# Folding beta1 in as a row-sum multiple on VectorE, broadcasting three constant rows on GpSimd, and reordering a planned schedule

## The chip, the cores and the metric

The kernel runs on one core of a Trainium2 chip. The core has TensorE (PE in the profile), VectorE (DVE), ScalarE (ACT), GpSimd (POOL), and SyncE (SP), which here only issues transfers. The metric is the device time of one execution in microseconds, and the time of a kernel is the median of its runs.

## The reference

A windowed attention with a few always-visible "sink" keys feeds a token-mixing and channel-mixing MLP block. B is 4, H 8, S 768, D 64, so the model width is 512. The window is 128 keys, there are 4 sinks, and the MLP's hidden width is 2048.

```python
scores = scale * np.matmul(q, k.transpose(0, 1, 3, 2))
keep = is_sink | in_window
a = np.exp(...); a = a / (np.sum(a, axis=-1, keepdims=True) + 1e-09)
x = np.matmul(a, v)                      # -> (B, S, H * D)

a1 = alpha1 * x + beta1
tok = np.einsum('ts,bsd->btd', w_tok, a1)
u = x + lam * tok
a2 = alpha2 * u + beta2
ch = np.maximum(a2 @ w_ch1, 0.0) @ w_ch2
out = u + lam * ch
```

The change concerns `lam * tok`. Written out, lam times w_tok applied to (alpha1 x + beta1) is w_tok applied to (lam alpha1 x), plus the row sum of w_tok at row t times (lam beta1). `lam`, `alpha1` and `beta1` are vectors over the 512 channels, so on chip they are needed as a row repeated in all 128 partitions.

## The kernel before, in words

**Work.** The four batches run one after the other. Each batch has attention (transposed q and k, scores S, exponentials E, the product pv with v, normalised into x), token mixing (tok, giving u in place in x), an affine and a transpose (uT), a first MLP product with relu (h, hT), and a second one (ch), added into x and written out. Rows are tiled by 128 (six tiles r or ti); the 2048 hidden channels are tiled by 128 (16 tiles fi). While the MLP of batch b runs, the attention of batch b+1 runs between its matmuls. Only batch 0 has its attention alone, at the start; there it is also split in two halves of four heads (G = 0 and 1).

**Order.** Nothing is ordered by a scheduler on the chip. A `Plan` gathers tasks (`add`): each has a priority, the engines that may run it with a cost in ns, the tasks it comes after, and the buffers it uses. `emit` walks a model of the five engines and of the DMA rings, always takes the task that can start first (ties by priority), gives it an engine and a buffer, and writes its instructions. So each engine gets a fixed sequence, and an instruction that has to wait holds up all that follow it on its engine. A task with `port=True` is kept from overlapping with GpSimd work when it runs on VectorE. Where the model sees TensorE idle before 36 us, it fills the gap with idle matmuls (`idle`, line 308). `since` is an earliest time in the model; `ROWS` is 7500 ns.

**Constants.** `lam`, `alpha1` and `beta1` are loaded as one row each (lines 329 to 331). `spread_rows` (line 937) multiplies alpha1 and beta1 by lam on GpSimd within one partition (lines 938 and 940), and `spread` (line 756) repeats each of the three rows over 128 partitions by an fp32 matmul with a column of ones (line 759) and a copy out of PSUM. The results are `lam_b`, `la1_b` and `lb1_b`.

**Where beta1 enters.** For batch 0 GpSimd multiplies each half of x by `la1_b` (`half`, line 691), and tok adds one more matmul, the row sums of w_tok (`rsr`) against the row lam beta1 (`lb16`, line 790). The row sums come from ScalarE's cast of w_tok with an accumulator (line 737), are put in a column (line 741), turned by a matmul (line 744) and copied to `rsr` (line 753). For batches 1 to 3 GpSimd does two passes over each x tile: times `la1_b` (line 701), plus `lb1_b` (line 704); the result xh goes straight into tok.

**Lines to follow.** Casts and copies go through `copy` (lines 315 on ScalarE and 317 on the other two). `trans` (line 500) casts a q or k tile, transposes it on TensorE (line 521) and copies it out to qkT. `scores` gives S (line 612, a bias added by line 607), E (line 627) and on VectorE a mask (line 636). `pv` gives line 659 and the normalisation (lines 682 and 683). `tok` is line 786, its addition into x line 795, its cast to u16 the copy again. `cast_w2` multiplies the second MLP weight by `lam_b` (line 768), on VectorE or GpSimd. The first MLP weight is loaded from GpSimd's queue (line 480).

Of the kernel before, what the change touches and what calls it, by code (L numbers as in the profile page):

```python
# [13 lines left out]
P_ = 128  # L14
# [83 lines left out]
class Task:  # L98
    def __init__(self, prio, engs, fn, after, uses, mode, lands, port):
        self.prio, self.engs, self.fn, self.uses = prio, engs, fn, uses  # L100
        self.mode, self.lands, self.port = mode, lands, port
        self.needs = [a for a in after if a and a.seen is None]
        self.ready = max([0.0] + [a.seen for a in after if a and a.seen is not None])
        self.then = []
        self.seen = None


class Plan:


    def __init__(self, pools, homes, fill):
        self.tasks = []

        self.fill = fill
        self.pools = pools
        self.homes = {k: [0.0] * n for k, n in homes.items()}
        self.busy = {k: [False] * n for k, n in homes.items()}

    def add(self, prio, engs, fn, after=(), uses=(), mode=None, lands=None, port=False,
            since=0.0):  # L120


        t = Task(prio, engs, fn, after, uses, mode, lands, port)
        t.ready = max(t.ready, since)
        for b in uses:
            b.left += 1
        for a in t.needs:
            a.then.append(t)
        self.tasks.append(t)
        return t  # L130

    def emit(self):
        order = sorted(range(len(self.tasks)), key=lambda i: (self.tasks[i].prio, i))
        rank = {id(self.tasks[i]): r for r, i in enumerate(order)}
        waiting = {id(t): len(t.needs) for t in self.tasks}
        open_ = []
        free = {e: 0.0 for e in (PE, ACT, DVE, POOL, SP)}
        rings = Rings()

        def admit(t):  # L140
            bisect.insort(open_, (rank[id(t)], t), key=lambda x: x[0])

        def end(t, seen):
            t.seen = seen
            for b in t.uses:
                b.left -= 1
                b.freed = max(b.freed, seen)
                if b.left == 0:
                    self.busy[b.kind][b.home] = False
                    self.homes[b.kind][b.home] = b.freed  # L150
            for o in t.then:
                o.ready = max(o.ready, seen)
                waiting[id(o)] -= 1
                if not waiting[id(o)]:
                    admit(o)

        def pick():
            best = None
            for r, t in open_:
                at = t.ready  # L160
                for b in t.uses:
                    if b.t is None and b.home is None:
                        homes = [h for h, x in zip(self.homes[b.kind], self.busy[b.kind]) if not x]
                        n = sum(1 for o in t.uses if o.t is None and o.kind == b.kind)
                        if len(homes) < n:
                            at = None
                            break
                        at = max(at, sorted(homes)[n - 1])
                if at is None:
                    continue  # L170
                for e in t.engs:
# [3 lines left out]
                    key = (at_e, r, at_e + t.engs[e])  # L175
                    if best is None or key < best[0]:
                        best = (key, t, e)
            return best

        for t in self.tasks:  # L180
            if not waiting[id(t)]:
                admit(t)
# [3 lines left out]
        done = 0  # L186
        while done < len(self.tasks):
            best = pick()
            if best is None or landing <= best[0][0]:
# [5 lines left out]
            (start, r, _), t, e = best  # L195
            open_.remove((r, t))
            for b in t.uses:
                if b.t is None:
                    spare = [i for i, x in enumerate(self.busy[b.kind]) if not x]
                    b.home = min(spare, key=lambda i: self.homes[b.kind][i])  # L200
                    self.busy[b.kind][b.home] = True
                    pool, shape, dtype = self.pools[b.kind]
                    b.t = pool.tile(b.shape or shape, b.dtype or dtype,
                                    tag=f"{b.kind}_{b.home}", bufs=1, name=b.name)
            until, idle, took = self.fill
            n = int((start - max(free[PE], 900.0)) / (took if free[PE] > 4500.0 else 110.0))
            if e == PE and free[PE] < until and n > 0:
                free_d = [(h, i) for i, (h, x) in enumerate(zip(self.homes["d"], self.busy["d"])) if not x]
                if free_d and min(free_d)[0] <= free[PE]:
                    h = min(free_d)[1]  # L210
                    idle(self.pools["d"][0].tile(
                        [P_, 512], FP32, tag=f"d_{h}", bufs=1, name=f"idle{done}"), n)
                    self.homes["d"][h] = start
                    mode = None
            t.fn(e)
# [12 lines left out]
            t.at = (e, start, free[e])  # L228
            done += 1
# [6 lines left out]
        self.ends = free  # L236


@with_exitstack
def kernel(  # L240
# [85 lines left out]
    rsr = Buf("tmp", [P, NR, P], FP16, "rsr")  # L326
    lb16 = Buf("tmp", [P, DM], FP16, "lb16")
# [15 lines left out]
    ones_r = const.tile([1, P], FP32, name="ones_r")  # L343
    nc.vector.memset(ones_r, 1.0)

    rcol = const.tile([P, S // P, P], FP16, name="rcol")
    nc.vector.memset(rcol, 0.0)
# [62 lines left out]
    SPREAD = -790  # L410
# [12 lines left out]
    def load_qk(p, b, hp, t, wait=None):  # L423
        bf = nat[b, hp, t] = Buf("nat", None, None, f"nat{b}_{hp}_{t}")
        src = (q, k)[t][b, 2 * hp : 2 * hp + 2]
        if b < XB:
            src = src.rearrange("h (p r) d -> p h (r d)", p=P)
            done["nat", b, hp, t] = add(
                p, {SP: 480}, lambda e: nc.sync.dma_start(bf.t, src), [wait], [bf], lands=(16, 72))
# [214 lines left out]
    def pv(p, b, r, G):  # L644
# [52 lines left out]
        elif G == 1:  # L697
            tmp = Buf("tmp", None, None, f"tmp{b}_{r}")

            def m1(e):  # L700
                nc.gpsimd.tensor_mul(tmp.t, bx.t.rearrange("p h d -> p (h d)"), la1_b)  # L701

            def m2(e):
                nc.gpsimd.tensor_add(bh.t, tmp.t, lb1_b)  # L704

            a = add(p + 0.2, {POOL: 1270}, m1, [a, done["x", b, r, 0], done["la1"]], [bx, tmp])
            done["xh", b, r, 1] = add(p + 0.3, {POOL: 1305}, m2, [a, done["lb1b"]] + prior, [tmp, bh])
# [17 lines left out]
    def cast_wtok(p, ti):  # L725
# [3 lines left out]
        pr = Buf("d", [P, P], FP32, f"rs{ti}")  # L729
        col = Buf("rec", [P, 1], FP32, f"rc{ti}")  # L730
# [5 lines left out]
        def cast(e):  # L736
            nc.scalar.activation(
                w.t.rearrange("p r i -> p (r i)"), src.t[:, ti % 3, :], AF.Copy, accum_out=col.t)

        def mid(e):  # L740
            nc.vector.tensor_copy(rcol[:, ti, 0:1], col.t)

        def row(e):
            nc.tensor.matmul(pr.t, rcol[:, ti, :], iden, start=True, stop=True)

        c_ = add(p, {ACT: 850}, cast, [done["wtn", ti]], [src, w, col])
        a = add(p + 0.1, {PE: 330}, tr, [c_], [w, pt])
        a = done["wtokT", ti] = add(
            p + 0.2, {DVE: 560, ACT: 810}, lambda e: copy(e, wtokT[:, :, ti * P : (ti + 1) * P], pt.t),
            [a], [pt])  # L750
        a = add(p + 0.25, {DVE: 146}, mid, [c_], [col])
        a = add(p + 0.3, {PE: 60}, row, [a], [pr])
        done["rs", ti] = add(p + 0.4, {DVE: 200, ACT: 280},
                             lambda e: copy(e, rsr.t[:, ti, :], pr.t), [a], [pr, rsr])

    def spread(p, name, src, o):

        pt = Buf("d", None, None, f"b_{name}")
        a = add(p, {PE: 900}, lambda e: nc.tensor.matmul(pt.t, ones_r, src, start=True, stop=True),  # L759
                [done.get(name)], [pt], since=ROWS)  # L760
        done[name] = add(p + 0.1, {DVE: 600, ACT: 600}, lambda e: copy(e, o, pt.t), [a], [pt])
# [15 lines left out]
    def tok(p, b, ti):  # L777
# [5 lines left out]
        def mm(sis):  # L783
            def f(e):
                for si in sis:
                    nc.tensor.matmul(  # L786
                        pt.t, wtokT[:, si, ti * P : (ti + 1) * P], hs[si].t,
                        start=(si == 0), stop=(si == NR - 1 and b > 0))
                if b == 0 and sis[-1] == NR - 1:
                    nc.tensor.matmul(pt.t, rsr.t[:, ti, :], lb16.t, start=False, stop=True)  # L790
# [10 lines left out]
        for sis in ((0, 1, 2, 3), (4, 5)) if b == 0 and ti < 2 else (range(NR),):  # L801
            after = [done["wtokT", ti], a, b == 0 and done["rs", ti], b == 0 and done["lb1"]] + [
                done["xh", b, r, G] for r in sis for G in ((0, 1) if b == 0 else (1,))]
            a = add(p, {PE: 215 * (len(sis) + (b == 0 and sis[-1] == NR - 1))}, mm(sis), after, [pt] + [hs[si] for si in sis] + [rsr, lb16] * (b == 0 and sis[-1] == NR - 1))
        done["tok", b, ti] = a
        before = [done["xh", b, ti, G] for G in ((0, 1) if b == 0 else (1,))]
        a = done["u", b, ti] = add(p + 0.1, {DVE: 690}, ua, [a] + before, [pt, bx])
# [129 lines left out]
    def spread_rows():  # L937
        done["la1"] = add(-880, {POOL: 1270}, lambda e: nc.gpsimd.tensor_mul(rows[1], rows[1], rows[0]),
                          since=ROWS)
        a = done["lb1b"] = add(-878, {POOL: 1270}, lambda e: nc.gpsimd.tensor_mul(rows[2], rows[2], rows[0]),  # L940
                               since=ROWS)
        z = add(-990, {POOL: 400}, lambda e: nc.gpsimd.memset(lb16.t, 0.0), [], [lb16])
# [134 lines left out]
```

## Time and profile before

The median of 13 runs is 272.6 us (270.18 to 274.27). The profiled execution took 274.27 us, and its span from the first to the last instruction is 272.6 us, so 1.67 us lie around the span; that the span equals the median is chance.

| what | value |
|---|---|
| span, profiled execution | 272.6 us |
| time of that execution | 274.27 us |
| median of 13 runs | 272.6 us |
| TensorE busy | 262.2 us, 96% |
| VectorE busy | 144.2 us, 53% |
| ScalarE busy | 133.6 us, 49% |
| GpSimd busy | 109.3 us, 40% |
| granted TensorE clock, mean | 0.972 |
| first h matmul (end of batch 0's attention and token mixing) | 50.3 us |
| TensorE idle before 50 us / after | about 5.1 us / 1.1 us, and the end |

To read it: "busy" of an engine counts its own instructions; a busy TensorE includes the idle matmuls that the kernel itself puts there (72 of them, 6.8 us) and time at a lower clock, where the same matmul takes longer. A wait on an engine is told with what released it. The chain of waits goes back from the last instruction through whatever each step waited for.

### The profile page before, as it was taken

How to read it: one execution, taken by the hardware profiler on the slowest of the kernel's cores; microseconds unless marked ns; L12 is line 12 of the kernel's file. 1: busy time of each engine (PE TensorE's matmuls, PEld its weight loads, DVE VectorE, ACT ScalarE, POOL GpSimd, SP SyncE). 2: the span in 40 equal slices, each digit the busy share in tenths (PEclk: the TensorE clock that was granted, in tenths of full speed). 3: DMA queues.
4: the chain of work that ended last, by engine and by line, in shares of the span. 5: the costliest groups of instructions: out<-in, count | busy, mean ns of one | idle time of the engine just before them, and what ended most of it. 6: DMA issues, size and time to landing. Idle time of an engine off the chain costs nothing.

```text
span 272.6 us, 4880 instructions
## 1 busy us (share of the span) xinstructions
PE 262.2 (96%) x1904; PEld 141.3 (52%) x1904; DVE 144.2 (53%) x299; ACT 133.6 (49%) x222; POOL 109.3 (40%) x124
## 2 busy tenths in 40 slices
PE   7599999999999999899999999999999999999994
PEld 6235465665655554455655444555654445665441
DVE  4336666777888744448996144279853344000222
ACT  3266877578755222688960023787700135773000
POOL 5741893692684472025886602004846000000000
PEclk9856999999999999999999999999999999999998
DMA  6999999908972897789956999200011233000221
GB/s 208 328 203 379 381 287 256 165 2 223 317 155 46 169 261 163 138 192 242 185 76 142 253 166 216 76 2 0 2 38 42 96 89 84 2 0 0 81 77 77
DMA packets 85485, 39.65 MB, mean 145 GB/s; under 512 B 73419, under 2 KB 79571, under 8 KB 85462
## 3 DMA queue, kind: packets, MB, share of 16 engines
q1 hardware_dynamic: 83328, 37.24, 54.8%
q0 software_dynamic: 2112, 2.10, 4.5%
q8 instruction: 15, 0.25, 0.4%
q14 instruction: 8, 0.07, 0.1%
q10 hardware_dynamic: 22, 0.01, 0.0%
HBM read 29.63 MB, written 6.29 MB: 132 GB/s over the span
## 4 chain that ended last, share of the span: by engine, by line
PE 92%; DMA 3%; DVE 2%; issue 1%; SPq 0%; ACT 0%; DVEq 0%; ACTq 0%
PE ch L893 30%; PE h L869 30%; PE tok L786 11%; PE S L612 5%; PE pv L659 4%; DMA nat<-in_k_dram 3%; PE tp L521 2%; PE S L607 2%; PE pv L652 1%; DVE E L636 1%; PE b_lb1b L759 1%; PE b_la L759 1%; PE b_lam L759 1%; PE sk L560 1%; PE wT L734 1%
## 5 line engine op out<-in xcount | busy, mean ns | idle before, releaser
L869 PE MATMUL h<-uT,w1f 128*128 128x384 f16 x512 | 90.7, 326 | 1.1 <-ACT uT L813 0.9
L893 PE MATMUL ch<-w2f,hT 128*128 128x512 f16 x384 | 88.4, 379 | 0.0
L869 PEld LDWEIGHTS <-w1f 128*128 128x128 f16 x512 | 47.4, 98 | 33.6 <-issue 4.8
L893 PEld LDWEIGHTS <-hT 128*128 128x128 f16 x384 | 36.4, 98 | 41.0 <-issue 0.2
L875 ACT ACTIVATE hT<-h 128x384 f16<-128x384 f32 x93 | 45.7, 491 | 21.2 <-PE h L869 21.0
L627 ACT ACTIVATE E<-S 128x1024 f16<-128x1024 f32 (+1 forms) x42 | 40.6, 1003 | 10.2 <-PE S L612 5.8
L904 DVE TENSOR_TENSOR x<-x,ch 128x512 f32<-128x512 f32 x24 | 16.5, 687 | 50.4 <-PE ch L893 49.8
L701 POOL TENSOR_TENSOR tmp<-x,la_b 128x512 f32<-128x512 f32 x18 | 25.5, 1419 | 39.3 <-DVE x L683 37.1
L315 ACT CAST u<-x 128x512 f16<-128x512 f32 x18 | 11.1, 617 | 58.4 <-DVE x L795 58.4
L786 PE MATMUL tok<-xh,wtokT 128*128 128x512 f16 x144 | 34.7, 379 | 0.0
L795 DVE TENSOR_TENSOR x<-x,tok 128x512 f32<-128x512 f32 x24 | 16.5, 688 | 22.3 <-PE tok L786 19.0
L704 POOL TENSOR_TENSOR xh<-tmp,lb_b 128x512 f16<-128x512 f32 x18 | 25.5, 1414 | 1.3
L877 DVE TENSOR_SCALAR hT<-h 128x384 f16<-128x384 f32 x35 | 19.2, 554 | 11.7 <-PE h L869 11.4
L636 DVE TENSOR_TENSOR E<-E,maskn 128x1024 f16<-128x1024 f16 x25 | 23.8, 985 | 0.0
L317 POOL CAST vf<-vnat 128x512 f16<-128x512 f32 x18 | 12.2, 680 | 24.5 <-DMA vnat<-in_v_dram 22.7
L786 PEld LDWEIGHTS <-wtokT 128*128 128x128 f16 x144 | 13.8, 98 | 15.3
L683 DVE TENSOR_TENSOR x<-pv,rec 128x256 f32<-128x256 f32 x48 | 20.4, 424 | 1.7
L659 PEld LDWEIGHTS <-E 128*128 128x128 f16 x328 | 15.7, 98 | 6.3 <-issue 1.4
L659 PE MATMUL pv<-vf,E 128*128 128x65 f16 x328 | 18.7, 194 | 0.1
L317 POOL CAST n<-nat 128x768 f16<-128x768 f32 x17 | 14.0, 825 | 8.0 <-DMA nat<-in_q_dram 3.9
L317 POOL CAST u<-x 128x512 f16<-128x512 f32 x6 | 3.7, 622 | 27.1 <-DVE x L795 20.7
L612 PE MATMUL S<-qkT 64*128 64x256 f16 (+1 forms) x168 | 14.3, 283 | 0.0
(101 smaller groups left out, 215.7 us busy)
## 6 DMA issues: line engine op xcount, KB each, us to landing
nat<-in_q_dram SPq DMA_DIRECT2D x16, 384.0 KB, 6.5
nat<-in_k_dram SPq DMA_DIRECT2D x16, 384.0 KB, 3.8
out_dram<-x SPq DMA_DIRECT2D x24, 256.0 KB, 2.2
vnat<-in_v_dram SPq DMA_DIRECT2D x18, 256.0 KB, 3.4
wst_w<-in_moe_w_ch_dram SPq DMA_DIRECT2D x8, 512.0 KB, 9.1
wtn<-in_moe_w_tok_dram SPq DMA_DIRECT2D x6, 384.0 KB, 5.1
w1f<-in_moe_w_ch_dram POOLq DMA_DIRECT2D x4, 512.0 KB, 14.0
v<-in_v_dram SPq DMA_DIRECT2D x12, 128.0 KB, 5.5
```

The source lines that it names most:

```text
L317: engine[e].tensor_copy(o, i)
L612: nc.tensor.matmul(pv_[:, e_, i, :], o.t[rows, 2 * hp + 1, j * P : (j + 1) * P], o.t[rows, 2 * hp, j * P : j * P + w], start=not bias, sto ...
L627: nc.scalar.activation(eT.t, pS.t[:, :, 0 : n * w].rearrange("p e (i w) -> p e i w", i=n), AF.Exp, scale=scale)
L636: nc.vector.tensor_mul(ev, ev, m.to_broadcast(list(ev.shape)))
L659: nc.tensor.matmul(po.t[:, hl, :], eT.t[:, e_, off + i, c : c + P], vf[j][:, h, :], start=(r < 2 and n == 0), stop=(n == len(parts) - 1 an ...
L683: nc.vector.tensor_mul(bx.t[:, 4 * G : 4 * G + 4, :], po.t[:, :, 0:D], rec.t.to_broadcast([P, 4, D]))
L701: nc.gpsimd.tensor_mul(tmp.t, bx.t.rearrange("p h d -> p (h d)"), la1_b)
L704: nc.gpsimd.tensor_add(bh.t, tmp.t, lb1_b)
L786: nc.tensor.matmul(pt.t, wtokT[:, si, ti * P : (ti + 1) * P], hs[si].t, start=(si == 0), stop=(si == NR - 1 and b > 0))
L869: nc.tensor.matmul(ph.t, w1f[:, c, fi * P : (fi + 1) * P], bu.t[:, c, chk * NTOK : (chk + 1) * NTOK], start=(c == 0), stop=(c == NC - 1))
L875: nc.scalar.activation(bh.t[:, fi, :], ph.t, AF.Relu)
L893: nc.tensor.matmul(pc.t, bh.t[:, fi, nt * P : (nt + 1) * P], w2f[:, fi, :], start=(fi == 0), stop=(fi == NF - 1))
```

## The change

Seven things are changed at once.

1. The three rows are repeated over the partitions by GpSimd (`partition_broadcast`) in place of three matmuls and copies, and the products with `lam` are then taken on full tiles (128x512) by VectorE or GpSimd in place of single rows on GpSimd.
2. beta1 leaves the token product. The row-sum matmul and copies, `rsr`, `lb16` and the extra matmul of batch 0 go; for all batches a VectorE instruction per tile adds row sum times `lb1_b` to x in place (`beta`), after xh has been made from x. The addition of tok waits for it.
3. GpSimd's two passes per tile of batches 1 to 3 become one (`full`).
4. The cast of w_tok may run on VectorE too, with its accumulator; the row sums stay in fp32, one column per tile.
5. The q/k cast number 2 goes from GpSimd to VectorE; two of the first loads have longer transfer costs in the model (85 and 140 in place of 72); `LO`, from where the attention of batch 1 is spread over batch 0's MLP, goes from 6 to 9.
6. `emit` is split into `run`, which only plans, and the writing of what was planned.
7. Before planning, the priorities go through `shuffle` once per seed of `TURNS`: about one in a hundred of the priorities of a group gets a random offset.

```diff
-    def emit(self):
+    def run(self, prio):
...
+    def emit(self, turns):
+
+        prio = [t.prio for t in self.tasks]
+        for seed in turns:
+            prio = shuffle(prio, seed)
+        for t, e, start, stop, idle in self.run(prio):
...
+            t.fn(e)
+
+
+def shuffle(prio, seed):
+
+    rnd = random.Random(seed)
+    lo = rnd.choice((-2200.0, -2200.0, -1000.0, -1000.0, 0.0, 50.0, 100.0))
+    hi = lo + (1300.0 if lo < -1500.0 else (1000.0 if lo < 0.0 else 60.0))
+    wide = 300.0 if lo < 0.0 else 10.0
+    return [p + rnd.gauss(0.0, wide) if lo <= p < hi and rnd.random() < 0.01 else p for p in prio]
...
-    rsr = Buf("tmp", [P, NR, P], FP16, "rsr")
-    lb16 = Buf("tmp", [P, DM], FP16, "lb16")
+    rsum = const.tile([P, NR], FP32, name="rsum")
...
-    SPREAD = -790
+
+    TURNS = (9002, 9013, 9165, 9291, 9475, 10035, 10043, 10361, 10426)
...
-                p, {SP: 480}, lambda e: nc.sync.dma_start(bf.t, src), [wait], [bf], lands=(16, 72))
+                p, {SP: 480}, lambda e: nc.sync.dma_start(bf.t, src), [wait], [bf], lands=(16, {(0, 0, 1): 85, (0, 1, 0): 140}.get((b, hp, t), 72)))
...
-            tmp = Buf("tmp", None, None, f"tmp{b}_{r}")
-
-            def m1(e):
-                nc.gpsimd.tensor_mul(tmp.t, bx.t.rearrange("p h d -> p (h d)"), la1_b)
-
-            def m2(e):
-                nc.gpsimd.tensor_add(bh.t, tmp.t, lb1_b)
-
-            a = add(p + 0.2, {POOL: 1270}, m1, [a, done["x", b, r, 0], done["la1"]], [bx, tmp])
-            done["xh", b, r, 1] = add(p + 0.3, {POOL: 1305}, m2, [a, done["lb1b"]] + prior, [tmp, bh])
+            def full(e):
+                engine[e].tensor_mul(bh.t, bx.t.rearrange("p h d -> p (h d)"), la1_b)
+
+            done["xh", b, r, 1] = add(
+                p + 0.3, {POOL: 1270}, full, [a, done["x", b, r, 0], done["la1"]] + prior, [bx, bh], port=True)
+        if G == 1:
+            def beta(e):
+                xf = bx.t.rearrange("p h d -> p (h d)")
+                engine[e].scalar_tensor_tensor(
+                    out=xf, in0=lb1_b, scalar=rsum[:, r : r + 1], in1=xf, op0=ALU.mult, op1=ALU.add)
+
+            done["xb", b, r] = add(
+                (1.5 if r < 3 else 4.5) if b == 0 else p + 0.4, {DVE: 640}, beta,
+                [done["xh", b, r, g] for g in ((0, 1) if b == 0 else (1,))] + [done["rs", r], done["lb1b"]],
+                [bx], port=True)
...
+            o, i_ = w.t.rearrange("p r i -> p (r i)"), src.t[:, ti % 3, :]
+            if e == ACT:
+                nc.scalar.activation(o, i_, AF.Copy, accum_out=rsum[:, ti : ti + 1])
+            else:
+                nc.vector.tensor_scalar(
+                    out=o, in0=i_, scalar1=1.0, scalar2=0.0, op0=ALU.mult, op1=ALU.add,
+                    accum_out=rsum[:, ti : ti + 1])
+
+        a = done["rs", ti] = add(p, {ACT: 850, DVE: 870}, cast, [done["wtn", ti]], [src, w])
...
-    def spread(p, name, src, o):
-
-        pt = Buf("d", None, None, f"b_{name}")
-        a = add(p, {PE: 900}, lambda e: nc.tensor.matmul(pt.t, ones_r, src, start=True, stop=True),
-                [done.get(name)], [pt], since=ROWS)
-        done[name] = add(p + 0.1, {DVE: 600, ACT: 600}, lambda e: copy(e, o, pt.t), [a], [pt])
...
-                        start=(si == 0), stop=(si == NR - 1 and b > 0))
-                if b == 0 and sis[-1] == NR - 1:
-                    nc.tensor.matmul(pt.t, rsr.t[:, ti, :], lb16.t, start=False, stop=True)
+                        start=(si == 0), stop=(si == NR - 1))
...
-        a = done["u", b, ti] = add(p + 0.1, {DVE: 690}, ua, [a] + before, [pt, bx])
+        a = done["u", b, ti] = add(p + 0.1, {DVE: 690}, ua, [a, done["xb", b, ti]], [pt, bx])
...
+    def fold_rows():
+        for i, (name, o) in enumerate((("lam", lam_b), ("a1", la1_b), ("b1", lb1_b))):
+            done[name] = add(
+                (-2041, -881, -850)[i], {POOL: 690},
+                lambda e, i=i, o=o: nc.gpsimd.partition_broadcast(o, rows[i]), since=ROWS)
+        done["la1"] = add(-880, {DVE: 640, POOL: 1270}, lambda e: engine[e].tensor_mul(la1_b, la1_b, lam_b),
+                          [done["lam"], done["a1"]], port=True)
+        done["lb1b"] = add(-825, {POOL: 1270, DVE: 640}, lambda e: engine[e].tensor_mul(lb1_b, lb1_b, lam_b),
+                           [done["lam"], done["b1"]], port=True)
...
-        cast = {DVE: 560} if i in (0, 1, 3, 7) else {POOL: 829}
+        cast = {DVE: 560} if i in (0, 1, 2, 3, 7) else {POOL: 829}
...
-    LO = 6
+    LO = 9
...
-    plan.emit()
+    plan.emit(TURNS)
```

## The prediction

> **What bounds the kernel now.** I read the chain of waits first, whose shares by engine are on the page.
>
> ```profile
> PE 92%; DMA 3%; DVE 2%; issue 1%; SPq 0%; ACT 0%; DVEq 0%; ACTq 0%
> ```
>
> TensorE sets the end. After the first h matmul (50.3 us) it is idle for about 1.1 us in 218 us, so an engine with spare time there buys nothing, and whatever ends batch 0's start earlier moves the rest with it, if inputs keep up. So the second view is the same chain in order of time (start, length, what):
>
> ```profile
> 10.92 0.51 PE tp L521 x6
> 11.42 1.87 PE b_lam L759 x2
> 13.30 0.33 PE vsp L579
> 13.62 2.00 PE b_la L759 x2
> 15.62 0.97 PE S L612 x8
> 16.59 0.54 PE sk L560 x2
> 17.13 2.00 PE b_lb1b L759 x2
> ```
>
> The three broadcast matmuls stand on the chain itself. Third, stretches of time (busy us of PE, PEld, DVE, ACT, POOL, then the granted clock):
>
> ```profile
> 10.00:20.00 10.00, 9.29 (x32) 3.24 (x32) 3.84 (x7) 5.20 (x11) 6.78 (x11) 0.58 0.98 240
> 20.00:30.00 10.00, 10.00 (x91) 4.83 (x89) 7.18 (x16) 6.95 (x11) 3.53 (x6) 0.74 1.03 380
> ```
>
> TensorE is full, the other engines are not, and the clock is at half (by single microseconds: 0.50 from 12 to 25 us). The DMA share beside it is about 1.0 (0.98, 1.03).
>
> **The change, part by part.** *Broadcasts off TensorE:* 1.87 + 2.00 + 2.00 = 5.87 us on the chain. *Row sums in the token product*, by TensorE's timeline:
>
> ```profile
> 40.34 0.38 PE L790 MATMUL tok<-lb,rsr 128*128 128x512 f16 x1
> 40.56 0.50 PE L734 MATMUL wT<-iden,wt 128*128 128x128 f16 x6
> 40.89 0.22 PE L744 MATMUL rs<-iden,rcol 128*128 128x128 f16 x1
> 40.95 1.03 PE L786 MATMUL tok<-xh,wtokT 128*128 128x512 f16 x4
> ```
>
> Matmuls overlap, so start to start counts: 0.22 for the added matmul, 0.06 for the turn of a row sum; six of each are 1.3 + 0.36, together 1.7. Off TensorE: 5.9 + 1.7 = 7.6 us.
>
> *Given back in the start.* S at 15.62 needs the last copy into qkT, which ends on VectorE at 11.46 + 0.96 = 12.42; so of the 3.87 us of two broadcasts ahead of it only 3.2 come through: 0.7 back. ScalarE is busy 10.6 of 13 us from 25 to 38; with that stretch about 1.7 shorter and E on the way to each pv, I put 1.0 for its queueing. GpSimd's twelve halves of xh (0.72 each, from 25.8 to 39.2) have 10.3 busy of the same 13 us: 0.8 more. Sum 2.5; bounds 0 (TensorE was last everywhere) and 5.5 (feeders leave only 2.1).
>
> *GpSimd's broadcasts.* The trace has none. Removed with them: a memset of 0.51 and the two row products. GpSimd's timeline:
>
> ```profile
> 8.39 0.82 POOL L317 CAST n<-nat 128x768 f16<-128x768 f32 x1 [3.26 <-DMA nat<-in_q_dram]
> 9.18 1.26 POOL L938 TENSOR_TENSOR row<-row,row 1x512 f32<-1x512 f32 x1
> 10.41 1.58 POOL L940 TENSOR_TENSOR row<-row,row 1x512 f32<-1x512 f32 x1
> ...
> 25.81 0.73 POOL L692 TENSOR_TENSOR xh<-x,la_b 128x256 f16<-128x256 f32 x1 [6.89 <-DVE x L683]
> ```
>
> A broadcast writes 128x512 from one row: no less than 0.51 (memset of 128x512 halves), no more than 1.58 (the slower row product); nearest is the cast of 128x512, 0.68. Three are 2.0 (1.5 to 4.7) against 3.35 removed. The first products on full tiles cost 0.74 on VectorE or 1.35 on GpSimd (line 768's rows) and are due only at 25.8, when `half` first reads `la1_b`. Behind the broadcasts in GpSimd's queue stand the casts of q/k pairs 4 to 6 (12 to 14.6 us) and six casts of v (15.3 to 18.9); TensorE's transposes and pv wait for those. Cast 4 ends at 12.76 and its transpose starts at 19.07: 6.3 us of cover, of which the shortened start uses up to 5.9. A new kind of GpSimd operation may need its code loaded, and again when the old kind returns; the nearest row is ScalarE's table load, 1.28. Two would be 2.6, inside the idle 3.26 and 6.89 shown. I take 0 on the path; bounds 0 and, with the rival below, more.
>
> [...]
>
> *VectorE's `beta`, GpSimd's single pass.* Rows by shape:
>
> ```profile
> L636 DVE TENSOR_TENSOR E<-E,maskn 128x1024 f16<-128x1024 f16 x25 | 23.8, 985 | 0.0
> L704 POOL TENSOR_TENSOR xh<-tmp,lb_b 128x512 f16<-128x512 f32 x18 | 25.5, 1414 | 1.3
> L768 DVE TENSOR_TENSOR w2f<-wst_w,lam_b 128x512 f16<-128x512 f32 x10 | 6.9, 738 | 0.0
> ```
>
> `beta` reads two fp32 tiles from SBUF, as line 768 on VectorE does: 0.74. Bounds: 0.69 (line 795, one input in PSUM) and 1.15 (a mask beside GpSimd work). 24 x 0.74 = 17.8 us, 13.3 of it in batches 1 to 3. Removed there: 18 x 1.41 = 25.5 us of GpSimd. A mask takes 0.68 alone and 0.985 on average; 25 x 0.30 = 7.6 us are contention with GpSimd, and with one of its two passes gone I take half back, 3.8. Net 9.5, or 3.2 a batch. VectorE's fullest stretches:
>
> ```profile
> 120.00:140.00 20.00, 20.00 (x189) 11.87 (x188) 17.43 (x34) 17.43 (x26) 13.77 (x13) 1.00 0.98 189
> 180.00:200.00 20.00, 20.00 (x196) 11.94 (x195) 17.81 (x38) 13.83 (x20) 9.21 (x7) 1.00 0.01 2
> ```
>
> have 2.57 and 2.19 us free, so up to 0.6 and 1.0 spill over, and masks, relus and normalisations stand behind. Part of each pv sequence falls after them (VectorE 1.8 of 5 us from 155 to 160), so I take 0.5 for both; bounds 0 and 4.
>
> [...]
>
> *Moved.* `beta` needs xh, the row sum and `lb1b`; behind it on VectorE stand masks and relus, and the u addition of its tile. In batch 0 its priority is past the token matmuls, and the casts with row sums run before those anyway: 0. Cast 2 on VectorE costs 0.55, in its idle 3.84 before 9.54. w_tok's cast on VectorE: a 768-wide cast there takes 0.55 to 1.32 against 0.84 on ScalarE: a wash. The longer load costs, `LO` and the shuffles change every engine's sequence; no DMA is added or taken away, and SP's queue may be permuted. What they can win after 50 us is the 1.1 us idle at 110.9, and they can lose as much: 0.
>
> Sum: -7.6 + 2.5 + 0 + 0.5 = -4.6 on the profiled span, 272.6 to 268.0. That execution took 274.27, so a like one would take 269.7; the median of the 13 runs is 1.67 below the profiled execution, so I predict **268.0** as the median.
>
> **Rivals.** *GpSimd's queue takes the place of the matmuls (slower).* If the broadcast holds GpSimd for long at 5 to 9 us and again at the return to ordinary products, casts 4 to 6, the v casts and the halves are late, and TensorE, in order, stops at a transpose. Cover is 0.4 (6.3 less 5.9) at the first place; the second has 6.89 less the 5.9 by which x comes earlier, 1.0. The gain of 4.6 is used up when the late time past both covers exceeds 4.6, so from some 6 us of hold-up in all. Held at both places for as long as GpSimd idles ahead of the first half, 2 x 6.89 = 13.8, it is 13.8 - 1.4 - 4.6 = 7.8 over; GpSimd's queue has some 2.7 of 13 us free to catch up (25 to 38 us), and what is planned around it about as much again, which leaves 3 to 4 over 272.6: **276.5**. For: an operation that the trace has never timed, in an in-order queue, by rows of only distant kin. Against: 10 us idle in the two places.
>
> *VectorE or the feeders decide.* With the upper ends, 5.5 for the start in place of 2.5, the sum is -1.6: **271.0**; with 4 us from VectorE in place of 0.5, -1.1: 271.5. For: 87 to 89% busy, DMA share 1.0. Against: w_tok's last load is issued at 20.7 and lands some 5.1 later, eight us before its first cast at 33.7.
>
> *The clock stays up (faster).* TensorE idles from 7.04 to 9.27 and the clock falls at 11.6; it stays at half until 25 whatever runs. The longer load cost of pair (0,1,0) makes the planner put idle matmuls there. Of the 13.5 us at half clock 7.6 remain without the broadcasts; at full clock 3.8 less: **264.2**. Against: feeders then bind sooner.
>
> *The shuffled order is better in the model alone:* the sum loses a us or two, inside the range.
>
> **How the numbers follow.** Forecast (266 to 270.3) 0.42; clock 0.13; VectorE or feeders 0.20 (270.3 to 272.5); GpSimd 0.25 (273 and up). Half a per cent, about what this kernel's measurement can tell, is 1.36 us: below 271.24 lie the first two and a third of the third, 0.62; same 0.13; slower 0.25. Cut off below 264 (0.06) and above 277 (0.10), the range is 264 to 277; the forecast's own is 266 to 270.3.
>
> **What would show it.** Right: no line 759 in the chain; S starting near 12.5; h starting at 45 to 46.5; `beta` at 0.74; VectorE under 95% at 120 to 140. Wrong: GpSimd's first `half` after 27 us, or a transpose waiting on a GpSimd cast; h at 50 or later; a clock still at half to 25 us and TensorE idle ahead of S; idle on TensorE after 50 us growing past 2 us with a mask or `beta` as releaser.

## Result, and the profile after

The changed kernel is slower. Its median is 275.29 us (11 runs, 273.68 to 277.84) beside 272.3 us for the kernel before on the same chip (48 runs, 269.66 to 274.27); the ratio is 1.0126, 95% interval 1.0096 to 1.0155. Ratios, here and below, are taken over the runs classed as fast alone (that of 277.84 is not), and differ by up to 0.5% from the quotients of the medians. The range of 264 to 277 holds it, the side does not: the GpSimd rival (276.5) came true.

The span of the profiled execution is 273.6 us. A span is TensorE's busy time plus its idle time, which sorts the kernels at a glance. The profiled execution of the kernel before was its longest (274.27 us), that of the changed kernel took its median, so the spans differ by 1.0 us where the medians differ by 3.0:

| kernel | span | TensorE busy | TensorE idle |
|---|---|---|---|
| before | 272.6 | 262.2 | 10.4 |
| after | 273.6 | 256.5 | 17.1 |

So the work did come off TensorE (5.7 us busy), and more than that came back as idle time (6.7 us). The shares by engine of the chain of waits after:

```profile
PE 82%; DVE 7%; SPq 4%; DMA 3%; issue 2%; POOL 1%; ACT 0%; DVEq 0%; ACTq 0%
```

TensorE had 92% of it before. The same chain in order of time (start, length, what) shows where it left TensorE:

```profile
15.26 3.52 DMA v<-in_v_dram
18.79 2.36 issue
21.14 1.25 POOL lb_b L953
22.39 0.79 POOL n L343
...
23.22 0.82 PE tp L542 x6
```

Read it from the bottom: a transpose waits for a GpSimd cast, that cast for GpSimd's product into `lb_b`, and that product, for 2.36 us, for "issue", which is no instruction of any engine that this view names. GpSimd's timeline (start, length, engine, line, operation, out<-in, tile, and in brackets the idle time before it and its releaser):

```profile
3.83 0.19 POOL L406 TENSOR_SCALAR_AFFINE_SELECT iden<-iden 8x8 f32<-8x8 f32 x1
11.23 0.80 POOL L950 PARTITION_BROADCAST lam_b<-row  x1 [7.21 <-issue]
11.91 0.80 POOL L950 PARTITION_BROADCAST la_b<-row  x1
12.57 0.80 POOL L950 PARTITION_BROADCAST lb_b<-row  x1
21.14 1.25 POOL L953 TENSOR_TENSOR lb_b<-lb_b,lam_b 128x512 f32<-128x512 f32 x1 [7.77 <-issue]
22.36 2.36 POOL L343 CAST n<-nat 128x768 f16<-128x768 f32 x3
24.67 3.35 POOL L343 CAST vf<-v 128x256 f16<-128x256 f32 x6
31.21 2.78 POOL L713 TENSOR_TENSOR xh<-x,la_b 128x256 f16<-128x256 f32 x4 [3.19 <-DVE rec L703]
```

Two gaps with no work: 7.21 us ahead of the first broadcast and 7.77 us ahead of the first product after the last one. The broadcasts take 0.80 each, 0.67 from start to start. All nine casts stand behind the second gap in the plan. In TensorE's timeline that gap is one wait:

```profile
11.97 0.68 PE L633 MATMUL S<-qkT 64*128 64x256 f16 x8
...
23.22 0.82 PE L542 MATMUL tp<-iden,n 128*128 128x128 f16 x6 [9.81 <-POOL n L343]
...
53.79 1.46 PE L878 MATMUL h<-uT,w1f 128*128 128x384 f16 x8 [0.24 <-DVE uT L824]
```

S starts at 11.97, 3.65 us earlier than before; h starts at 53.79, 3.5 us later. A lower clock comes on top of the wait, as the windows show (busy us of PE, PEld, DVE, ACT, POOL, then the granted clock, DMA share and GB/s):

```profile
17.00:18.00 1.00, 0.00 (x0) 0.00 (x0) 0.00 (x0) 0.00 (x0) 0.00 (x0) 0.90 1.06 233
18.00:19.00 1.00, 0.00 (x0) 0.00 (x0) 0.00 (x0) 0.00 (x0) 0.00 (x0) 0.50 1.08 233
...
24.00:27.00 3.00, 3.00 (x17) 0.93 (x16) 2.92 (x4) 1.02 (x1) 3.00 (x6) 0.50 1.03 394
27.00:28.00 1.00, 1.00 (x10) 0.59 (x10) 0.41 (x1) 0.38 (x1) 1.00 (x2) 0.50 1.06 378
28.00:29.00 1.00, 1.00 (x14) 0.44 (x11) 0.70 (x1) 1.00 (x2) 0.02 (x1) 0.98 1.07 373
```

TensorE starts again at 23.2 at half clock, which lasts until 28: 4.8 us of work at a clock of 0.50, some 2.4 us lost by estimate (half of 4.8) beside the 9.8 us of idling. In the three other kernels with this broadcast (below) the clock is low beside the long waits of TensorE too: where one is 27.20 us, 0.50 in two stretches between 20.50 and 38.47 us; where one is 7.75, 0.65 from 30 to 40 us; where one of 6.06 is followed by one of 8.62, 0.65 from 21.0 to 32.7 us. A long wait is not needed for it: in the kernel with the matmul broadcasts put back (also below) the mean clock is 0.69 from 10 to 20 us, with no wait of TensorE over 1.4 us.

### The profile page after: what moved, and what is told of

The parts are those of the page before. It is cut to its first block, busy times and chain, and to the rows that moved or that the text cites. A ratio compares the mean times of both kernels' runs of the same rounds, so it can differ in the third digit from the quotient of the medians.

```text
span 273.6 us, 4903 instructions
## 1 busy us (share of the span) xinstructions
PE 256.5 (94%) x1921; PEld 141.7 (52%) x1921; DVE 147.5 (54%) x302; ACT 140.7 (51%) x231; POOL 78.5 (29%) x102
## 4 chain that ended last, share of the span: by engine, by line
PE 82%; DVE 7%; SPq 4%; DMA 3%; issue 2%; POOL 1%; ACT 0%; DVEq 0%; ACTq 0%
PE h L878 30%; PE ch L902 28%; PE tok L798 9%; PE pv L680 4%; PE S L633 4%; SPq L477 3%; PE S L628 2%; DVE x L727 2%; PE pv L673 2%; PE tp L542 1%; DMA v<-in_v_dram 1%; DVE w2f L780 1%; DMA nat<-in_k_dram 1%; DVE E L657 1%; SPq L450 1%
## 5 line engine op out<-in xcount | busy, mean ns | idle before, releaser
L902 PE MATMUL ch<-w2f,hT 128*128 128x512 f16 x384 | 89.8, 379 | 0.0
L878 PE MATMUL h<-uT,w1f 128*128 128x384 f16 x512 | 87.8, 326 | 0.2 <-DVE uT L824 0.2
L884 ACT ACTIVATE hT<-h 128x384 f16<-128x384 f32 x108 | 52.9, 492 | 19.3 <-PE h L878 18.8
L720 POOL TENSOR_TENSOR xh<-x,la_b 128x512 f16<-128x512 f32 x18 | 24.5, 1360 | 52.7 <-DVE x L704 36.1
L727 DVE SCALAR_TENSOR_TENSOR x<-lb_b,rsum,x 128x512 f32<-128x512 f32 x24 | 19.7, 838 | 2.1 <-POOL xh L720 2.1
L886 DVE TENSOR_SCALAR hT<-h 128x384 f16<-128x384 f32 x20 | 11.1, 555 | 17.1 <-PE h L878 16.9
L657 DVE TENSOR_TENSOR E<-E,maskn 128x1024 f16<-128x1024 f16 x25 | 19.8, 808 | 0.2 <-ACT E L648 0.2
L542 PE MATMUL tp<-iden,n 128*128 128x128 f16 x96 | 9.1, 241 | 10.2 <-POOL n L343 9.8
L341 ACT CAST n<-nat 128x768 f16<-128x768 f32 x14 | 11.4, 829 | 9.9 <-DVE x L913 9.9
L343 POOL CAST n<-nat 128x768 f16<-128x768 f32 x13 | 11.3, 884 | 10.3 <-DMA nat<-in_q_dram 8.3
## 6 DMA issues: line engine op xcount, KB each, us to landing
out_dram<-x SPq DMA_DIRECT2D x24, 256.0 KB, 2.7
vnat<-in_v_dram SPq DMA_DIRECT2D x18, 256.0 KB, 3.8
w1f<-in_moe_w_ch_dram POOLq DMA_DIRECT2D x4, 512.0 KB, 10.4
```

What stands on the lines that cost most here:

```text
L341: nc.scalar.copy(o, i)
L343: engine[e].tensor_copy(o, i)
L657: nc.vector.tensor_mul(ev, ev, m.to_broadcast(list(ev.shape)))
L720: engine[e].tensor_mul(bh.t, bx.t.rearrange("p h d -> p (h d)"), la1_b)
L727: engine[e].scalar_tensor_tensor(out=xf, in0=lb1_b, scalar=rsum[:, r : r + 1], in1=xf, op0=ALU.mult, op1=ALU.add)
L878: nc.tensor.matmul(ph.t, w1f[:, c, fi * P : (fi + 1) * P], bu.t[:, c, chk * NTOK : (chk + 1) * NTOK], start=(c == 0), stop=(c == NC - 1))
```

## The experiments

**Theory.** GpSimd is held for 7 us or more each time it turns to `partition_broadcast` and each time it turns back to ordinary two-input products, and the casts queued behind stop TensorE. **Rivals:** the gaps are waits for landing loads; VectorE's new `beta` costs the time; the new order does. One fact speaks for the theory ahead of any experiment. The trace holds pairs of MODIFY_POOL_CONFIG on GpSimd's sequencer (POOLq), which the timeline above leaves out: one in the kernel before (ahead of the first affine_select, line 337, at 0.9 us), three in the kernel after (there, line 362, at 1.2 us; ahead of the first broadcast; and ahead of the first product after the last). By source line, the broadcasts (line 950) and the product (line 953) show (ns min/median/max, then first and last start):

```profile
L950 POOLq MODIFY_POOL_CONFIG  x2: 1/1/1, 4.0 to 4.0; - x2
...
L953 POOLq MODIFY_POOL_CONFIG  x2: 127/127/127, 13.3 to 13.3; - x2
```

They stand where the two gaps begin, at 4.0 and 13.3 us. The pair ahead of the first affine_select is followed by its operation within 0.2 us in both kernels: not every such pair has a gap behind it. An expectation below says "by no instruction"; that is so of the 7 us, not of their start. Nothing in the queues of the profile stands for the rest of a gap: the two instruction queues have 15 and 8 packets in both kernels.

The ratios below are to the kernel before, run on the same chip along with each group of experiments (medians 271.40 to 271.74).

**More turns, same order.** The alpha1 product, which VectorE took, goes between the second and the third broadcast on GpSimd.

```diff
+    def spread(i, o):
+        if i == 2:
+            nc.gpsimd.tensor_mul(la1_b, la1_b, lam_b)
+        nc.gpsimd.partition_broadcast(o, rows[i])
...
-        done["la1"] = add(-880, {DVE: 640, POOL: 1270}, lambda e: engine[e].tensor_mul(la1_b, la1_b, lam_b),
...
+        done["la1"] = add(-880, {DVE: 640, POOL: 1270}, lambda e: None,
```

> The changed kernel with the alpha1 product taken on GpSimd between the second and the third broadcast (VectorE took it before), same order otherwise and the same results; GpSimd now turns from one kind of operation to the other four times in place of two. Theory (each turn holds GpSimd for 7 to 8 us, by no instruction): four gaps of about 7 to 13 us in its timeline, at each turn, the first half of xh near 46 in place of 31, and 287 to 300 us. Rival (GpSimd waits for something else at that time, the landing loads above all, and a turn costs nothing or is paid once): two gaps as before and one more 1.3 us product, 275 to 278 us.

Measured: 292.93 us, ratio 1.0798 (1.0735 to 1.0860). GpSimd's timeline of this kernel, and below it the stretches of its four gaps, with the columns of the windows above:

```profile
10.94 0.80 POOL L949 PARTITION_BROADCAST lam_b<-row  x1 [6.92 <-issue]
...
19.25 1.25 POOL L948 TENSOR_TENSOR la_b<-la_b,lam_b 128x512 f32<-128x512 f32 x1 [6.83 <-issue]
30.55 0.80 POOL L949 PARTITION_BROADCAST lb_b<-row  x1 [10.05 <-issue]
38.47 1.25 POOL L958 TENSOR_TENSOR lb_b<-lb_b,lam_b 128x512 f32<-128x512 f32 x1 [7.12 <-issue]
39.69 2.36 POOL L343 CAST n<-nat 128x768 f16<-128x768 f32 x3
```

```profile
4.02:10.94 6.92, 6.07 (x91) 5.34 (x89) 3.13 (x8) 3.21 (x5) 0.00 (x1) 1.00 1.07 330
12.42:19.25 6.83, 0.93 (x12) 0.43 (x8) 0.00 (x0) 2.40 (x3) 0.00 (x1) 0.70 1.04 225
20.50:30.55 10.05, 0.00 (x0) 0.00 (x0) 0.00 (x0) 0.00 (x0) 0.01 (x1) 0.50 0.89 324
31.35:38.47 7.12, 0.00 (x0) 0.00 (x0) 0.00 (x0) 0.00 (x0) 0.01 (x1) 0.50 0.00 0
```

Each turn makes a gap. In the last one no engine works and no recorded transfer runs (0 GB/s), and it still takes 7.12 us: it is a wait for no input and no other engine. The four gaps are 30.9 us in all, 15.9 more than the changed kernel's two, 17.2 with the added product; TensorE's wait for the transpose grows from 9.81 to 27.20 us, and the median is 17.6 us above the changed kernel's (18.3 by the two ratios): with nothing left to cover them, the further turns go into the time whole. The rival of landing loads falls.

**The turn moved.** Same order, the beta1 product on VectorE, so that GpSimd's next two-input product is the first `half`.

```diff
-                           lambda e: engine[e].tensor_mul(lb1_b, lb1_b, lam_b),
+                           lambda e: nc.vector.tensor_mul(lb1_b, lb1_b, lam_b),
```

> Every engine's order as in the changed kernel, but the product lb1_b * lam_b runs on VectorE instead of GpSimd. Theory (GpSimd is held for some 7.5 us before its first partition broadcast and again before the next two-input product after it, as for loading code): the second hold moves behind the nine casts, to just before the first half of xh; the casts follow the broadcasts at once, the transpose that waited until 23.2 us runs at about 14 to 15, the first half still starts late (26 to 28 us against 31.2), and the median falls by 3 to 5 us, to 270 to 272.5. Rival (GpSimd is held because the lb1_b product itself waits for something, or by transfers): with the product gone from its queue the second hold disappears, the first half runs at 22 to 23 us and the time falls by 8 or more. Second rival (the late casts do not decide): within 1 us of 275.3.

Measured: 277.76 us, ratio 1.0216 (1.0136 to 1.0296): the place was right, but the time rose by 2.5 us over the changed kernel's where a fall of 3 to 5 was expected. GpSimd's timeline, then TensorE's:

```profile
16.87 3.35 POOL L343 CAST vf<-v 128x256 f16<-128x256 f32 x6
33.02 4.12 POOL L713 TENSOR_TENSOR xh<-x,la_b 128x256 f16<-128x256 f32 x6 [12.79 <-issue]
37.09 0.74 POOL L343 CAST vf<-v 128x256 f16<-128x256 f32 x2
```

```profile
37.53 0.54 PE L680 MATMUL pv<-vf,E 128*128 128x65 f16 x7 [7.75 <-POOL vf L343]
```

The casts run before the gap now, so they need no turn; the product does. But the gap grew to 12.79 us and stops pv through two casts of v behind it. In it the transfers moved 370 GB/s.

**The broadcast alone.** The kernel before with nothing changed but the broadcasts on GpSimd and, with them, the products with `lam` on full tiles, planned anew.

```diff
-        spread(-879, "la1", rows[1], la1_b)
-        spread(SPREAD, "lb1b", rows[2], lb1_b)
-        spread(SPREAD + 1, "lam", rows[0], lam_b)
+        for i, (name, o) in enumerate((("lam", lam_b), ("a1", la1_b), ("b1", lb1_b))):
+            done[name] = add(
+                (-2041, -881, -850)[i], {POOL: 690},
+                lambda e, i=i, o=o: nc.gpsimd.partition_broadcast(o, rows[i]), since=ROWS)
...
```

> The kernel before with the GpSimd broadcast alone: the rows are spread by GpSimd and multiplied on full tiles, all else as before (beta1's row for batch 0 is copied from the spread tile), planned anew. Theory: two holds of 7 us or more on GpSimd, one before the first broadcast and one before the next two-input GpSimd product; 3 to 8 us slower than before, 275 to 280. Rival (the broadcast is harmless, the other parts cost): within 1.5 us of before.

Measured: 285.04 us, ratio 1.0553 (1.0473 to 1.0633): more than the 275 to 280 expected, and this part alone, in an order of its own, makes the kernel slower than the whole change does. Its gaps on GpSimd's timeline are 7.70 and 11.72 us (the timeline puts the first down to a load of v, as it puts the first gap of the experiment above, 7.67 us, down to one of q; that these two are turns is read from their place, right ahead of the first broadcast, and their size), and TensorE waits 6.06 us for a cast of q/k and 8.62 us for one of v:

```profile
32.72 1.25 POOL L935 TENSOR_TENSOR la_b<-la_b,lam_b 128x512 f32<-128x512 f32 x1 [11.72 <-issue]
```

**All but the broadcast.** The changed kernel with the matmul broadcasts of before put back, planned anew with the same seeds.

```diff
-        for i, (name, o) in enumerate((("lam", lam_b), ("a1", la1_b), ("b1", lb1_b))):
...
+        spread(-879, "la1", rows[1], la1_b)
+        spread(-790, "lb1b", rows[2], lb1_b)
+        spread(-789, "lam", rows[0], lam_b)
```

> The changed kernel with the three rows multiplied on GpSimd and spread by fp32 matmuls as before; beta1 as a row-sum multiple, the single GpSimd pass, and the shuffled priorities stay, and the plan is made anew. Theory (only the GpSimd broadcast costs): no hold on GpSimd, the broadcasts take 3 to 6 us of TensorE while it waits for loads anyway, h starts at 47 to 50 us, median 268 to 271.5. Rival (the beta part or the order is what costs): 273 or more.

Measured: 269.13 us, ratio 0.9924 (0.9888 to 0.9960). As expected (268 to 271.5). In this order the rest of the change is worth 2.1 us, and the broadcast on GpSimd takes it back with 3.4 more.

**Rows by transfers, late.** Same order as after; at the places of the broadcasts ScalarE's queue issues transfers that read a row into all partitions.

```diff
-                lambda e, i=i, o=o: nc.gpsimd.partition_broadcast(o, rows[i]), since=ROWS)
+                lambda e, i=i, o=o: nc.scalar.dma_start(o, (moe_lam, moe_alpha1, moe_beta1)[i].partition_broadcast(P)),
+                since=ROWS)
```

> Every engine's order as in the changed kernel, but the three rows are spread over the partitions by three broadcast transfers from ScalarE's queue at the places of GpSimd's three broadcasts. No GpSimd operation of a new kind is left. Theory: both holds of GpSimd (7.2 and 7.8 us of idle time with no releaser) are gone, TensorE's 9.8 us wait for the transpose shrinks to under 3, S and pv run some 8 us earlier, and the median is 266 to 269. Rival (the start was bound by transfers all along): the holds go, but casts and pv wait for loads instead, and the time stays above 271.

Measured: 273.61 us, ratio 1.0098 (1.0064 to 1.0133). The time is the rival's (above 271), but the run tells less than it was meant to, because it has a delay of its own. TensorE's wait for the transpose did shrink (2.66 us), but a new one of 5.76 us stands ahead of it, for a cast of v on ScalarE. ScalarE's three issues end at 11.0, 14.2 and 16.7 us, its other work is idle for 2.3 us up to the first and for 4.9 us around the other two, and GpSimd's product is as late as after:

```profile
22.13 1.26 POOL L951 TENSOR_TENSOR lb_b<-lb_b,lam_b 128x512 f32<-128x512 f32 x1 [18.30 <-DMA v<-in_v_dram]
```

Here the releaser is a load, there it was "issue": the same late product from two causes. The third row was issued at 16.4 us and landed 5.6 us later, right ahead of the product that reads it.

**Without `beta`, and without shuffles.** Both take the kernel with late transfers: one leaves beta1 out in batches 1 to 3, the other plans with no seeds.

```diff
+                if b == 0:
+                    engine[e].scalar_tensor_tensor(
...
-    TURNS = (9002, 9013, 9165, 9291, 9475, 10035, 10043, 10361, 10426)
+    TURNS = ()
```

> As the kernel with rows by transfers, and in batches 1 to 3 the VectorE instruction that adds row sum times lam*beta1 is left out (so beta1 is missing from the token product there). Theory (VectorE's added work is mostly covered): 0 to 1.5 us less than the kernel with rows by transfers. Rival (VectorE decides in the middle batches): 3 us or more less, and masks and relus start earlier between 80 and 100 and 140 and 160 us.

> As the kernel with rows by transfers, planned without the nine seeded shuffles. Theory (the shuffles refine the model's order only): within 1.5 us of it, either way. Rival (they carry a real gain): 2 us or more slower than it.

Measured: without `beta` 273.25 us, ratio 1.0058 (1.0018 to 1.0097), which is 0.36 us less by the medians and 1.1 by the ratios, whose intervals overlap; VectorE's busy time falls from 147.2 to 134.6 us. So most of the 12.6 us of VectorE's work is covered, the rival's 3 us or more did not come, and it falls too. Without shuffles 275.69 us, ratio 1.0159 (1.0092 to 1.0226), 2.1 us more by the medians and 1.7 by the ratios, whose intervals overlap: the shuffled order is not the cause.

**Rows by transfers, first of all.** Same order as after, no broadcast on GpSimd; the three row loads, ScalarE's first instructions, write all partitions themselves.

```diff
-    for o_, i_ in zip(rows, (moe_lam, moe_alpha1, moe_beta1)):
-        nc.scalar.dma_start(o_, i_.unsqueeze(0))
+    for o_, i_ in zip((lam_b, la1_b, lb1_b), (moe_lam, moe_alpha1, moe_beta1)):
+        nc.scalar.dma_start(o_, i_.partition_broadcast(P))
...
-                lambda e, i=i, o=o: nc.gpsimd.partition_broadcast(o, rows[i]), since=ROWS)
+                lambda e: None, since=ROWS)
```

> Every engine's order as in the changed kernel, but the three rows are spread by broadcast transfers that ScalarE's queue issues first of all, so that they are there long before GpSimd's product; no GpSimd broadcast is left, and nothing waits for one. Theory (GpSimd's two holds are the whole loss): GpSimd's product runs by 10 us, the casts of pairs 4 to 6 by 13, TensorE has no wait over 3 us before S of the second half, the first h matmul starts at 45 to 47 us in place of 53.8, and the median is 266 to 269. Rival (the start is bound by transfers, and the 0.79 MB more makes it worse): h starts after 50 us and the median stays above 271.

Measured: **267.22 us, ratio 0.9867 (0.9814 to 0.9920)**, faster than both kernels and as expected. On GpSimd's timeline the product stands at 9.26 and the halves from 24.09 (31.21 after); the casts of q and k, expected by 13, run from 14.46:

```profile
9.26 1.26 POOL L952 TENSOR_TENSOR lb_b<-lb_b,lam_b 128x512 f32<-128x512 f32 x1 [5.42 <-DMA nat<-in_k_dram]
14.46 2.94 POOL L343 CAST n<-nat 128x768 f16<-128x768 f32 x3 [3.94 <-DVE n L343]
...
24.09 2.09 POOL L712 TENSOR_TENSOR xh<-x,la_b 128x256 f16<-128x256 f32 x3 [2.10 <-DVE rec L702]
```

S starts late, at 16.89 (11.97 after): these transfers are issued from 0.80 to 2.20 us, and the loads of k and q take longer to land, 5.8 and 7.2 us in the median of all 16 (4.7 and 5.7 after). TensorE: busy 256.0, idle 10.5, span 266.5. With the instructions otherwise in the same order, the two turns, less what the transfers cost in their place, therefore take 7.1 us of span (273.6 less 266.5), 6.6 of it idle, and 2.59% of the time, about 7.0 us. h starts at 46.59, and the clock is full in the stretch that ran at half before:

```profile
10.00:20.00 10.00, 9.56 (x116) 7.62 (x113) 4.44 (x8) 5.90 (x11) 4.79 (x8) 1.00 1.08 284
```

**Its order.** The same kernel with no shuffles; and with a plan made for it (broadcast tasks left out, the first load's cost at 225) and newly found seeds.

```diff
-    TURNS = (9002, 9013, 9165, 9291, 9475, 10035, 10043, 10361, 10426)
+    TURNS = ()
...
+    TURNS = (30034, 30038, 30508)
```

> The kernel with the three rows spread by the first transfers, planned with no shuffles. Theory (the shuffled order is worth about 2 us on the chip too, as it was where the broadcasts were late transfers): 268.5 to 270. Rival (the shuffles are better in the model alone): 266.5 to 268.

> The same rows by first transfers, with the three broadcast tasks out of the plan, the first load's modelled cost raised for the rows ahead of it, and three newly found shuffles. In the model it ends 5.3 us before the order of the recorded shuffles and 2.2 us before none. Theory (a plan that matches what runs is better by a part of that): 264.5 to 267. Rival (TensorE is full after the start in any of these orders, and the start is bound by the loads): 267 to 269.

Measured: without shuffles 271.28 us, ratio 0.9986 (0.9957 to 1.0016); with the new order 269.97 us, ratio 0.9948 (0.9923 to 0.9974). Both theories and both rivals missed. The recorded shuffles are worth 1.2%, some 3.2 us. The new order, 5.3 us better in the model, is 0.8% worse on the chip. Without shuffles TensorE runs below full clock in the start (0.73 in this window, 1.00 above) and h starts at 49.18:

```profile
10.00:20.00 10.00, 10.00 (x103) 7.85 (x101) 3.02 (x7) 5.10 (x9) 4.35 (x6) 0.73 0.97 258
```

**Row transfers from SyncE's queue.** The rows come at places in SyncE's plan, everything planned anew.

```diff
+    def load_row(p, name, o, i_):
+        done[name] = add(p, {SP: 480}, lambda e: nc.sync.dma_start(o, i_.partition_broadcast(P)),
+                         lands=(8, 90))
```

> The changed kernel with the rows spread by transfers in SyncE's own queue, lam and alpha1 after the first half's v and beta1 after the second half's, planned anew with these costs. Theory: no hold on GpSimd, nothing of it in front of the casts, h starts at 45 to 49 us, median 266 to 270. Rival (transfers bind): the 0.79 MB push w_tok and the second half's v back by 2 us and the median stays above 271.

Measured: 272.46 us, ratio 1.0051 (1.0017 to 1.0085), a miss on the rival's side of 271. h starts at 43.32, earliest of all, but TensorE is idle 3.0 us between 80 and 100 us, mostly waiting for a normalisation of pv, and is busy 257.9 in all. An early h of another order is no gain by itself.

## Why the prediction failed, point by point

**The step that failed** is "GpSimd's broadcasts": "the nearest row is ScalarE's table load, 1.28. Two would be 2.6, inside the idle 3.26 and 6.89 shown. I take 0 on the path". The count of two was right, the size was not: 7.21 and 7.77, 15.0 us in all, almost six times the 2.6. The cover was misjudged as well. The idle of 3.26 and 6.89 was there in the order of before; in the new one all casts stand behind both gaps. The nearest row in kind, a table load of another engine, was not near in size.

**The size of a turn.** That code may have to be loaded for a new kind of operation was the author's supposition; no run shows what is done in a gap. What the runs show is the size, 6.83 to 12.79 us in ten gaps, and that it is paid on the way back to two-input products too (7.77 us). No instruction stands for the wait itself; a pair of MODIFY_POOL_CONFIG stands at its start in the changed kernel. The error was to let a row of another engine, 1.28 us, set the size for this one.

**The GpSimd rival** had the place, both gaps ("2 x 6.89 = 13.8", measured 15.0) and the end (276.5, measured 275.3). That 276.5 is so near has luck in it: the rival's own terms, 7.8 less 2.7 and "about as much again", leave 2.4 over 272.6 and not the 3 to 4 written, so 275.0. Its covers were not what decided: it came as one wait of 9.81 us at a transpose, with the clock's 2.4 us behind it, and the two turns together cost 7.0 us of time against a gain of 3.6 without them (both by the ratios).

**Broadcasts and row sums off TensorE (7.6, 2.5 given back).** TensorE's busy time is 5.7 us lower although its idle matmuls rose from 6.8 to 9.6 us, so 8.5 of other busy time went. Part of that is the clock and not work: TensorE was busy at half clock for some 13.5 us before and 4.8 after. How much of the saving reaches the end depends on the order: with the rows by first transfers and the recorded seeds the kernel gains 3.6 us by the ratio (4.2 by the medians), not far from the 4.6 of the sum; with no seeds it gains 0.4, which can't be told from nothing. So the 4.6 was nearly met, but some 3.2 us of it are the shuffles', for which the prediction had "0". What is left for "-7.6 + 2.5" is small; since the row transfers have their own price in these kernels (S 4.9 us later), no run shows how much of these two terms was wrong.

**`beta`.** By shape, in the changed kernel (busy us, then mean ns):

```profile
L657 DVE TENSOR_TENSOR E<-E,maskn 128x1024 f16<-128x1024 f16 x25 | 19.8, 808 | 0.2 <-ACT E L648 0.2
L727 DVE SCALAR_TENSOR_TENSOR x<-lb_b,rsum,x 128x512 f32<-128x512 f32 x24 | 19.7, 838 | 2.1 <-POOL xh L720 2.1
L780 DVE TENSOR_TENSOR w2f<-wst_w,lam_b 128x512 f16<-128x512 f32 x12 | 8.8, 775 | 0.0
```

Predicted 0.74, measured 0.838 on average, and 0.74 for many single ones. The masks went from 985 to 808 ns, which gives 25 x 0.177 = 4.4 us back (predicted 3.8). The plain product of line 780, a full tile too, takes 0.775 on average. The 0.5 for both stands within what the run without `beta` can tell (0.36 or 1.1); no run shows the upper bound of 4. VectorE's fullest stretches did fill:

```profile
80.00:100.00 20.00, 19.83 (x176) 10.55 (x174) 19.05 (x37) 7.91 (x10) 7.97 (x8) 1.00 0.62 120
...
140.00:160.00 20.00, 20.00 (x182) 10.53 (x181) 18.65 (x38) 9.16 (x11) 10.11 (x8) 1.00 0.61 137
```

95% and 93% busy, at other places than foreseen, with TensorE still full beside them.

**The clock rival** (264.2) is half right: with no gap the clock is 1.00 from 10 to 20 us in the kernel of 267.22. In the changed kernel it was 1.00 until 17 us and 0.50 from 18, during the wait; that the wait took it is read from the order of events, not from a run made for it, and the kernel with the matmul broadcasts put back has 0.69 from 10 to 20 us without such a wait.

**Of the signs named**, "a transpose waiting on a GpSimd cast", "first `half` after 27 us" (31.2) and "h at 50 or later" (53.8) all came; "S starting near 12.5" came too (11.97), a sign of the forecast that says nothing about the end. So did VectorE under 95% from 120 to 140 us (5.29 of 20), where its work no longer stood.

**Open.** Why some gaps take 10 to 13 us: the three of them (10.05, 11.72, 12.79) stand beside 324 to 375 GB/s, but others of 6.92 and 7.21 beside 330 and 342, so traffic alone does not settle it. What the recorded shuffles have that the model does not see was not tried.

## What to carry to other kernels

An operation that an engine has not run in this kernel is priced by what it brings with it, not by its own 0.80 us: here each turn of GpSimd, to it or back from it, holds that engine for 6.83 to 12.79 us, and every cast queued behind it waits. If no row of the trace has the operation, a rival with a large price and an in-order queue behind it deserves most of the chance, and one small kernel that doubles the turns settles it. A row that is only to be repeated can be written so by the load itself, issued first (267.22 us here, beside 275.29), and a planned order is to be timed on the chip: here the model put one order 5.3 us ahead of another, and it ran 0.8% slower.

## What the runs showed of the hardware that was not expected

- A turn of GpSimd to `partition_broadcast`, or from it back to two-input products, holds it for 6.83 to 12.79 us (ten gaps in four kernels, the smallest in mid-traffic, 7.12 with the whole core at rest). At two of the ten, 7.67 and 7.70, the profile names a load as releaser. A pair of MODIFY_POOL_CONFIG of at most 0.13 us each stands at the start of both gaps of the changed kernel (4.0 and 13.3 us), shown by source line and not in the timeline; for the rest of a gap the profile has no instruction of GpSimd, and the two instruction queues have 15 and 8 packets as in the kernel before. Casts ran after a broadcast with no gap (at 13.67 us after the one at 13.03 in the kernel with the turn moved, at 16.86 between those at 16.20 and 17.24 in the one with the broadcast alone).
- `partition_broadcast` to 128x512 in fp32 takes 0.79 to 0.80 us (twelve of them in four kernels), 0.65 to 0.69 from start to start of one behind another.
- After a wait of 9.81 us on TensorE, the granted clock went to 0.50 at 18 us, 5 us into it, and came back only at 28 us, 4.8 us after work had begun again.
- Three row transfers issued from ScalarE at 10 to 17 us, with the DMA share at 1.05 from 10 to 20, left its other work idle for 2.3 us up to the first and 4.9 us around the other two; what held the issues is not shown. As its first instructions they end by 2.2 us, ahead of its first other work at 3.14, but the loads of k and q take 5.8 and 7.2 us to land in the median, in place of 4.7 and 5.7.
